# One core, attention and two feed-forward stages: the attention loop's scans, gate logits, row scatters and last two tiles put in another order and on other engines

## The chip, the cores and the metric

The kernel runs on one core of a Trainium2 chip. The metric is the device time of one execution in microseconds (us): 826.85 us before the change, median of 3 runs (826.71 to 828.07). The engines are TensorE (PE, with PEld for its weight loads), VectorE (DVE), ScalarE (ACT), GpSimd (POOL) and SyncE (SP, which only issues transfers here). Each runs its own instructions in order and waits on semaphores.

## The reference

A recurrent attention with per-channel decay is followed by a mixture of experts with one expert for each token, and that by a dense feed-forward layer. Cut to what matters:

```python
batch, n_heads, seq, head_dim = (4, 8, 768, 48)
for t in range(S):                       # w is drawn from 0.8 to 0.95
    cur = np.einsum('bhd,bhe->bhde', u[None] * kt, vt)
    y[:, :, t] = np.einsum('bhd,bhde->bhe', rt, state + cur)
    state = wt[:, :, :, None] * state + np.einsum('bhd,bhe->bhde', kt, vt)
x = y as (3072 tokens, 384)
logits = x @ w_gate;  e_idx = argmax(logits);  gate_w = softmax(logits)[e_idx]
eom = sigmoid(x @ w_output_gate)
out[token] = gate_w * eom[e_idx] * (relu(x @ w1[e_idx]) @ w2[e_idx])
h = out @ w_in;  result = (h * clip(h + 3, 0, 6) / 6) @ w_out
```

## The kernel before

**Stage one, attention.** The sequence is cut into chunks of 128 steps, and each chunk of one batch entry is a *tile*: 24 tiles (NT), numbered so that tile i continues tile i-4 (B = 4). In a tile the 8 heads lie in 4 pairs (PR = 4), a pair on 112 partitions. One load brings `a` (w with a zero column ahead of each pair's 128, then r, then k) and one brings `v`.

The recurrence of a chunk becomes matrix products. DVE scans w backward to R (`prep_a`: the product of all decays behind a step; its column 0 is the decay of the whole chunk) and forward to Fx. Before the forward scan the reciprocals of column 0 of R are put into the marks `mk_f`, so that Fx carries 1/(whole decay). GpSimd forms kh = k times R (`prep_k`), m = r times k (`prep_m`), sb = the carried state T times the decay; DVE forms rh = r times Fx (`prep_b`). Then PE makes scores `sc` from kh and rh (`scores`), DVE copies the causal part of them over the diagonal matrix A (two masked copies, L456), PE multiplies A by v and adds rh times sb (`ymm`, tile `yp`), ACT copies that out as `ys`. The state update goes over `kt` (a transpose, tile `kp`, copied to `ks` by ACT) and `upd` (tile `up`, then T on DVE).

**Gate and scatter.** `small_a` multiplies ys and m by the gate weights for all four pairs (`lt`, copied to `lts`), `small_b` transposes that (`lp`); DVE takes the diagonal terms `av` from it (L534), from which GpSimd makes the A of the next tile (affine select, L536), and sums the 16 logits over the pairs into `L` (L543). When a group of 4 (later 2) tiles is complete, some 16 small DVE instructions (`gate_steps`, `gate_pb`, `gate_b`) find each token's expert, its row there (`pi`) and its factor (`sg`). Then for each tile of the group PE transposes ys (`rows_pe`), GpSimd writes a token number (`rows_id`), ACT scales by sg into `xs` (`rows_act`, L640), and GpSimd issues an indirect transfer of the 128 rows to `x_w` in memory (`scatter`, L647). `clear` zeroes a window of `x_w` for each expert beforehand.

**The loop.** Step i prepares tile i+2, makes scores of tile i, `ymm` of tile i-1, logits of tile i-2. The order is written by hand (a manual schedule). Small gate instructions are woven into the next step by `tick`. PSUM tags are single buffers: `k` serves kp, up and lp; `x` serves the busy matmuls, lt and row transposes; `y` serves yp; `s0` and `s1` serve the scores. A matmul into a tag waits until the earlier tenant has been read. A *step* below runs from one backward scan (L392) to the next; step i scans tile i+2, so the scan of tile 23 begins step 21. After the loop the last tiles, two gates and eight scatters are written out by hand. In between, the weights of the first expert are split (`piece_hi` on ACT, `piece_lo` on DVE, 16 of each).

**Stages two and three** (experts, dense layer) start when all scatters have landed and the first window of `x_w` is loaded: the transposes at L872. From there PE is busy to the end. No instruction of these stages is changed.

Of the kernel before, what the change touches and what calls it, by code (L numbers as in the profile page):

```python
# [7 lines left out]
F32 = mybir.dt.float32  # L8
# [12 lines left out]
C = 128  # L21
# [191 lines left out]
def kernel(  # L213
# [33 lines left out]
    wg_sb = ca.tile([PP, 2, PR, 32], F32, name="wg_sb")  # L247
    rev8_s = ca.tile([128, E], F32, name="rev8_s")
# [114 lines left out]
    nc.gpsimd.memset(b_lo, W_LO)  # L363
# [21 lines left out]
    def prep_a(i):  # L385


        d = tl[i]
        tick()
        a = d["a"]  # L390
        R = wk.tile([PP, PR * SEG], F32, tag="R", name="R", bufs=3)
        nc.vector.tensor_tensor_scan(out=R[:, ::-1], data0=a[:, 1:1 + PR * SEG][:, ::-1], data1=mk_r[:, ::-1],  # L392
                                     initial=0.0, op0=ALU.mult, op1=ALU.max)
        tick()
        nc.vector.reciprocal(out=mk_f[:, 0:PR * SEG:SEG], in_=R[:, 0:PR * SEG:SEG])
        tick()
        Fx = wk.tile([PP, PR * SEG], F32, tag="F", name="Fx", bufs=3)
        nc.vector.tensor_tensor_scan(out=Fx, data0=a[:, 0:PR * SEG], data1=mk_f,
                                     initial=0.0, op0=ALU.mult, op1=ALU.add)
        tick()  # L400
        d["R"], d["F"] = (x.rearrange("p (a b) -> p a b", b=SEG) for x in (R, Fx))
# [126 lines left out]
    def small_b(i, j, lts):  # L528
        lp = ps_o.tile([128, 128], F32, tag="k", name="lp")
        nc.tensor.transpose(out=lp, in_=lts, identity=ident)  # L530
        lq = lp.rearrange("t (p q) -> t q p", p=PR)
        if j < NT:
            av = wk.tile([128, 2, PR], F32, tag="av", name="av")
            nc.vector.tensor_copy(av, lq[:, 16:18, :])  # L534
            A = wk.tile([128, 2, PR, C], F32, tag="A", name="A", bufs=4)
            nc.gpsimd.affine_select(out=A, in_=av.unsqueeze(3).to_broadcast([128, 2, PR, C]), pattern=[[0, 2], [0, PR], [1, C]],  # L536
                                    compare_op=ALU.is_equal, fill=0.0, base=0, channel_multiplier=-1)
            tl[j]["A"] = A
        if 0 <= i < NT:
# [690 lines left out]
```

## Time and profile before

| | |
|---|---|
| median of 3 runs | 826.85 us (826.71 to 828.07) |
| the profiled execution | 828.91 us |
| its span, first to last instruction | 827.1 us (1.8 us lie around it) |
| busy: PE, DVE, ACT, POOL | 781.5, 489.8, 351.0, 167.5 us |
| first transposes of stage two | 194.12 us after the span's start |

The profile is one execution. A row of its timeline gives start and duration of instructions of one line, the number of them merged, and in brackets the idle time of the engine before, with what ended it. Busy times of PE are modelled and overlap; durations of steps are therefore read from starts.

### The profile page before, as it was taken

Reading aid. Unit: us, or ns where it says so; the run is one execution under the profiler, and the core shown is the slowest. Engines: PE = TensorE matmul, PEld = TensorE weight load, DVE = VectorE, ACT = ScalarE, POOL = GpSimd, SP = SyncE. Lnnn points to the kernel's source line nnn. Section 1 sums busy time; section 2 is a strip of 40 time slices with the busy share of each in tenths; the row PEclk is TensorE's granted clock in tenths of the full one; section 3 lists DMA queues with packets and bytes.
Section 4 is the critical chain, followed back from the end, with each engine's and each line's share of the span. In section 5 each row is a group of like instructions: output and inputs, shape, how many; then the busy total and the mean of one; then the engine's idle time right before and its main releaser. Section 6 shows DMA issues by size and latency. Waiting matters only on the chain.

```text
span 827.1 us, 13670 instructions
## 1 busy us (share of the span) xinstructions
PE 781.5 (94%) x5349; PEld 694.3 (84%) x5359; DVE 489.8 (59%) x993; ACT 351.0 (42%) x671; POOL 167.5 (20%) x240
## 2 busy tenths in 40 slices
PE   6789989888999999999899999999999999999996
PEld 3567767667999999989889899999999999999995
DVE  7989999843776877787777633433343343343332
ACT  3445555532545555464554533333333333333332
POOL 5657888745000000000000020001002002002002
PEclk9999999989999999999999999999999999999998
DMA  9996675114568777575522010000001001001001
GB/s 248 295 284 193 187 205 163 41 68 158 190 184 214 179 261 208 169 155 195 148 84 59 1 38 2 1 4 35 0 1 39 1 2 38 1 1 39 1 1 42
DMA packets 31867, 85.47 MB, mean 103 GB/s; under 512 B 6521, under 2 KB 17985, under 8 KB 31793
## 3 DMA queue, kind: packets, MB, share of 16 engines
q1 hardware_dynamic: 28721, 75.05, 31.5%
q0 software_dynamic: 3072, 9.45, 3.1%
q8 instruction: 44, 0.72, 0.4%
q14 instruction: 30, 0.25, 0.1%
HBM read 67.11 MB, written 17.39 MB: 102 GB/s over the span
## 4 chain that ended last, share of the span: by engine, by line
PE 48%; issue 32%; DVE 10%; DMA 3%; POOL 3%; ACT 2%; SPq 0%; POOLq 0%; ACTq 0%; DVEq 0%
PE hp L879 6%; PE hp L880 6%; PE hp L881 6%; PE yp L880 3%; PE yp L879 3%; PE yp L881 3%; PE op L881 3%; PE op L880 3%; PE op L879 3%; PE yp L492 2%; POOL out_dram L1116 2%; PE sc L445 2%; DVE A L456 2%; PE yp L497 2%; DVE wlo L345 2%
## 5 line engine op out<-in xcount | busy, mean ns | idle before, releaser
L1030 DVE SCALAR_TENSOR_TENSOR t<-t,hp 128x512 f32<-128x512 f32 x96 | 66.0, 687 | 161.0 <-ACT t L1029 161.0
L1116 POOL DMA_INDIRECT out_dram<-ob,ids_sb x24 | 24.7, 1030 | 595.6 <-ACT ob L1114 590.5
L1029 ACT ACTIVATE t<-hp,b 128x512 f32<-128x512 f32 x96 | 65.9, 686 | 160.4 <-PE hp L881 153.9
L879 PE MATMUL op<-whi,hhi 128*128 128x384 f32 x380 | 128.4, 338 | 0.0
L880 PE MATMUL op<-wlo,hhi 128*128 128x384 f32 x380 | 128.3, 338 | 0.0
L881 PE MATMUL op<-whi,hlo 128*128 128x384 f32 x380 | 128.1, 337 | 0.0
L879 PE MATMUL hp<-xhi,win_hi 128*128 128x512 f32 x288 | 112.7, 391 | 1.9 <-ACT xhi L1017 1.9
L880 PE MATMUL hp<-xlo,win_hi 128*128 128x512 f32 x288 | 113.8, 395 | 0.4 <-DVE xlo L1018 0.4
L881 PE MATMUL hp<-xhi,win_lo 128*128 128x512 f32 x288 | 112.8, 392 | 0.0
L1036 DVE TENSOR_TENSOR hlo<-t,hhi 128x512 fp32r<-128x512 f32 x95 | 65.8, 693 | 66.3 <-ACT hhi L1035 66.3
L1035 ACT ACTIVATE hhi<-t 128x512 fp32r<-128x512 f32 x95 | 60.0, 632 | 72.2 <-DVE t L1030 72.2
L879 PEld LDWEIGHTS op<-whi,hhi 128*128 128x128 f32 x380 | 71.3, 188 | 4.1
L880 PEld LDWEIGHTS op<-wlo,hhi 128*128 128x128 f32 x380 | 71.2, 187 | 3.7
L345 DVE TENSOR_TENSOR wlo<-raw,whi 128x384 fp32r<-128x384 f32 x144 | 74.1, 551 | 0.0
L321 ACT ACTIVATE whi<-raw 128x768 fp32r<-128x768 f32 x64 | 53.9, 843 | 42.6 <-DMA raw<-in_w_dram 30.3
L881 PEld LDWEIGHTS op<-whi,hlo 128*128 128x128 f32 x380 | 71.2, 187 | 0.2 <-DVE hlo L1036 0.2
L879 PE MATMUL yp<-hhi,whi 128*128 128x360 f32 (+6 forms) x192 | 65.0, 339 | 3.1 <-ACT yst L1065 3.1
L879 PE MATMUL hp<-xhi,whi 128*128 128x360 f32 (+6 forms) x186 | 64.9, 349 | 0.5 <-ACT xhi L858 0.5
L880 PE MATMUL yp<-hlo,whi 128*128 128x360 f32 (+6 forms) x192 | 65.0, 339 | 0.1
L881 PE MATMUL yp<-hhi,wlo 128*128 128x360 f32 (+6 forms) x192 | 65.0, 339 | 0.0
L881 PEld LDWEIGHTS hp<-xhi,win_lo 128*128 128x128 f32 x288 | 54.1, 188 | 11.8
L880 PE MATMUL hp<-xlo,whi 128*128 128x360 f32 (+6 forms) x186 | 63.1, 339 | 0.8 <-DVE xlo L859 0.8
(169 smaller groups left out, 1405.2 us busy)
## 6 DMA issues: line engine op xcount, KB each, us to landing
raw<-in_w_dram SPq DMA_DIRECT2D x32, 768.0 KB, 5.3
a<-in_att_dram SPq DMA_DIRECT2D x23, 675.5 KB, 5.8
raw<-in_wout_dram SPq DMA_DIRECT2D x16, 384.0 KB, 6.8
raw<-in_win_dram SPq DMA_DIRECT2D x16, 384.0 KB, 4.5
v<-in_tok_dram SPq DMA_DIRECT2D x24, 192.0 KB, 9.6
wo_d<-v SPq DMA_DIRECT2D x16, 192.0 KB
raw<-wo_d SPq DMA_DIRECT2D x4, 768.0 KB, 4.1
xw<-x_w SPq DMA_DIRECT2D x4, 576.0 KB, 5.6
```

The costliest lines, as they stand in the source:

```text
L321: nc.scalar.activation(out=chunks[key][0][:, sl], in_=raws[key][:, sl], func=AF.Copy)
L345: nc.vector.tensor_tensor(out=lo[:, sl], in0=raws[key][:, sl], in1=hi[:, sl].bitcast(F32), op=ALU.subtract)
L445: nc.tensor.matmul(out=scs[hf][:, p, :], lhsT=kh[r0:r0 + D, p, :], rhs=rh[r0:r0 + D, p, :], start=True, stop=True)
L456: nc.vector.copy_predicated(out=d["A"][:, hf], mask=mask.unsqueeze(1).to_broadcast([128, PR, C]), data=scs[hf])
L879: nc.tensor.matmul(out=out_ap, lhsT=lh, rhs=rh, start=first, stop=False)
L880: nc.tensor.matmul(out=out_ap, lhsT=lh, rhs=rl, start=False, stop=False)
L881: nc.tensor.matmul(out=out_ap, lhsT=ll, rhs=rh, start=False, stop=last)
L1029: nc.scalar.activation(out=t, in_=hp, func=AF.Relu, bias=b_3)
L1030: nc.vector.scalar_tensor_tensor(out=t, in0=t, scalar=6.0, in1=hp, op0=ALU.min, op1=ALU.mult)
L1035: nc.scalar.activation(out=hi, in_=t, func=AF.Copy)
L1036: nc.vector.tensor_tensor(out=lo, in0=t, in1=hi.bitcast(F32), op=ALU.subtract)
L1116: ins = nc.gpsimd.indirect_dma_start(out=out, out_offset=bass.IndirectOffsetOnAxis(ap=ids_sb[:, i:i + 1], axis=0), in_=ob, in_offset=None)
```

## The change

The change touches stage one only.

- One tile of marks serves both scans: 1e-25, and 1.0 at the segment borders, shifted by a column for the forward scan, which now takes the maximum where it added. It no longer carries 1/(whole decay); its result `Fp` lies in PSUM. The reciprocals go to a small tile `rt`, and ACT multiplies r by them (`prep_s`, four activations of 128 columns, one for each pair). `rh` is the product of that (`rs`) and `Fp`.
- The logits and diagonal terms come from one matmul of lts with a constant `sel` (24 columns) in place of the transpose; it goes to tag `y`, and ACT copies it out. The DVE copy and reduction of `small_b` are gone.
- The lower check of w reads column 0 of R (4 columns) where it read 512 columns of w.
- `kt` is issued ahead of `prep_b`; scatters of a tile are issued right behind its rows, ahead of the affine select (`diag`); 3 busy matmuls stand in a gate step.
- The clears stand in steps 1 to 6 (two in each of steps 4 and 5) where they stood in 0 to 7; the raw weight loads and the splits by piece stand in other steps.
- The loop ends one step earlier, and the rest has a new order.

```diff
-    mk_r, mk_f = (vtile(PR * SEG)[0:PP] for _ in range(2))
+    marks = vtile(PR * SEG + C)[0:PP]
+    mk_r, mk_f = marks[:, 0:PR * SEG], marks[:, C:C + PR * SEG]
+    Fp = vtile(PR * SEG)[0:PP]
...
-        nc.vector.reciprocal(out=mk_f[:, 0:PR * SEG:SEG], in_=R[:, 0:PR * SEG:SEG])
+        nc.vector.reciprocal(out=rt, in_=d["R"][:, :, 0])
...
-        nc.vector.tensor_tensor_scan(out=Fx, data0=a[:, 0:PR * SEG], data1=mk_f,
-                                     initial=0.0, op0=ALU.mult, op1=ALU.add)
+        nc.vector.tensor_tensor_scan(out=Fp, data0=d["a"][:, 0:PR * SEG], data1=mk_f,
+                                     initial=0.0, op0=ALU.mult, op1=ALU.max)
...
+        for p in range(PR):
+            nc.scalar.activation(out=rs[:, p, :], in_=d["a"][:, WM + p * C:WM + (p + 1) * C], func=AF.Copy, scale=d["rt"][:, p:p + 1])
...
-        nc.vector.tensor_tensor(out=rh, in0=a[:, WM:WM + PR * C].rearrange("p (a b) -> p a b", b=C),
-                                in1=Fx[:, :, 0:C], op=ALU.mult)
+        nc.vector.tensor_tensor(out=rh, in0=d["rs"], in1=Fp.rearrange("p (a b) -> p a b", b=SEG)[:, :, 0:C], op=ALU.mult)
...
-        nc.tensor.transpose(out=lp, in_=lts, identity=ident)
...
-            nc.vector.tensor_copy(av, lq[:, 16:18, :])
...
-            nc.vector.tensor_reduce(out=gd[g]["L"][:, z, :], in_=lq[:, 0:2 * E, :], axis=AX.X, op=ALU.add)
+        lp = ps_o.tile([128, 24], F32, tag="y", name="lp")
+        nc.tensor.matmul(out=lp, lhsT=lts, rhs=sel, start=True, stop=True)
...
+        nc.scalar.activation(out=lq, in_=lp, func=AF.Copy)
...
-        if 0 <= i < E:
-            clear(i)
+        for e in CLEARS.get(i, ()):
+            clear(e)
...
-        keep_busy(NWARM[i + 3] if i < 2 else 1, ps_o, "x")
+        keep_busy(NWARM[i + 3] if i < 2 else 3 if gb is not None else 1, ps_o, "x")
...
+        av = small_v(i - 2, i + 1, small_p(lts)) if lts is not None else None
+        for z in range(0 if i < E else 1 if i < 20 else 2):
             if todo:
                 j = todo.pop(0)
-                rows_pe(j, ("x", "s1")[z])
+                rows_pe(j, ("x", "k")[z])
                 rows_id(j)
                 rows_act(j)
-                sq.append(j)
+                scatter(j)
...
+        if av:
+            diag(*av)
```

Where the instructions stand, on DVE, in step 12 of the loop, before (the row names a line, an operation, output and inputs; `vps` is the PSUM tile of the marks):

```order
L392 SCALAR_TENSOR_TENSOR R<-a,vps 112x516
L395 RECIPROCAL vps<-R 112x4
L398 SCALAR_TENSOR_TENSOR Fx<-a,vps 112x516
L456 COPY_PREDICATED A<-mask,sc_1392 128x512
L456 COPY_PREDICATED A<-mask,sc_1393 128x512
L422 TENSOR_TENSOR rh<-a,Fx 112x512
L480 TENSOR_TENSOR T<-up,sb 112x192
L345 TENSOR_TENSOR wlo<-raw,whi 128x384
L534 COPY av<-lp 128x8
L543 TENSOR_REDUCE vps<-lp 128x16
```

The same step on DVE with the change (`vps` now also holds Fp):

```order
L399 SCALAR_TENSOR_TENSOR R<-a,vps 112x516
L407 RECIPROCAL rt<-R 112x4
L409 SCALAR_TENSOR_TENSOR vps<-a,vps 112x516
L475 COPY_PREDICATED A<-mask,sc_1437 128x512
L475 COPY_PREDICATED A<-mask,sc_1438 128x512
L441 TENSOR_TENSOR rh<-rs,vps 112x512
L499 TENSOR_TENSOR T<-up,sb 112x192
L352 TENSOR_TENSOR wlo<-raw,whi 128x384
```

The last two rows are gone, and rh reads one operand from PSUM and one that ACT wrote.

On ACT, a step before, from the copy of kp on:

```order
L464 ACTIVATE ks<-kp 128x448
L500 ACTIVATE ys<-yp 112x512
L525 ACTIVATE lts<-lt 128x128
L640 ACTIVATE xs<-xp,sg 128x384
L435 ACTIVATE junk,wchk<-a,b_lo 112x512
L435 ACTIVATE junk,wchk<-a,b_hi 112x512
L340 ACTIVATE whi<-raw 128x384
```

And with the change:

```order
L483 ACTIVATE ks<-kp 128x448
L434 ACTIVATE rs<-a,rt 112x128 x4
L519 ACTIVATE ys<-yp 112x512
L544 ACTIVATE lts<-lt 128x128
L561 ACTIVATE L<-lp 128x24
L672 ACTIVATE xs<-xp,sg 128x384
L454 ACTIVATE junk,wchk<-R,b_lo 112x4
L454 ACTIVATE junk,wchk<-a,b_hi 112x512
L347 ACTIVATE whi<-raw 128x384
```

Five activations more stand in the step, four of them between ks and ys, and the first check is 4 columns wide.

On POOL, a step before (`gap` is a small write behind each scatter):

```order
L414 TENSOR_TENSOR kh<-a,R 112x512
L407 TENSOR_TENSOR m<-a 112x512
L427 TENSOR_TENSOR sb<-T,R 112x192
L633 COPY xs<-tokid 128x1
L536 AFFINE_SELECT A<-av 128x1024
L647 DMA x_w<-xs,pi 24576x385
L285 MEMSET gap 1x1
```

And with the change:

```order
L425 TENSOR_TENSOR kh<-a,R 112x512
L418 TENSOR_TENSOR m<-a 112x512
L445 TENSOR_TENSOR sb<-T,R 112x192
L665 COPY xs<-tokid 128x1
L679 DMA x_w<-xs,pi 24576x385
L292 MEMSET gap 1x1
L567 AFFINE_SELECT A<-L 128x1024
```

The affine select that makes the next tile's A now stands behind the scatter; in steps 20 and 21 it stands behind two of them.

## Rows read from the trace of the kernel before

**Rows 1.** Busy time by stretch: us, PE, PEld, DVE, ACT, POOL, PEclk, DMA share, GB/s.
```profile
13.66:64.52 50.86, 40.29 (x571) 30.71 (x578) 45.01 (x91) 22.69 (x59) 30.77 (x31) 0.90 0.97 285
64.52:132.00 67.48, 62.41 (x921) 47.79 (x920) 64.70 (x134) 36.95 (x92) 56.99 (x69) 0.97 0.68 189
132.00:154.87 22.87, 20.04 (x270) 15.30 (x268) 21.05 (x60) 12.48 (x35) 16.93 (x23) 0.90 0.32 103
154.87:194.12 39.25, 32.53 (x316) 22.48 (x315) 18.88 (x81) 12.02 (x31) 23.98 (x42) 0.89 0.22 77
```

**Rows 2.** Timeline of DVE: a gate step begins at 77.35, step 12 at 92.01.
```profile
77.35 1.22 DVE L392 TENSOR_TENSOR_SCAN R<-a,vps 112x516 f32<-112x516 f32 x1
...
85.72 1.20 DVE L392 TENSOR_TENSOR_SCAN R<-a,vps 112x516 f32<-112x516 f32 x1
...
92.01 1.23 DVE L392 TENSOR_TENSOR_SCAN R<-a,vps 112x516 f32<-112x516 f32 x1
...
97.97 0.15 DVE L534 COPY av<-lp 128x8 f32<-128x8 f32 x1
...
98.30 1.23 DVE L392 TENSOR_TENSOR_SCAN R<-a,vps 112x516 f32<-112x516 f32 x1
```

**Rows 3.** Timeline of PE, from logits transpose to logits transpose, one step.
```profile
97.59 0.33 PE L530 MATMUL lp<-ident,lts 128*128 128x128 f32 x1 [0.15 <-DVE T L480]
97.85 1.16 PE L445 MATMUL sc<-rh,kh 48*128 48x128 f32 x16
...
103.88 0.33 PE L530 MATMUL lp<-ident,lts 128*128 128x128 f32 x1 [0.16 <-DVE T L480]
```

**Rows 4.** The line of rh: duration ns min/median/max, first and last start.
```profile
L422 DVE TENSOR_TENSOR rh<-a,Fx x24: 661/921/1545, 7.1 to 158.7; 112x512 f32<-112x512 f32 x24
```

**Rows 5.** The same for the state update, one of whose inputs lies in PSUM.
```profile
L480 DVE TENSOR_TENSOR T<-up,sb x16: 340/349/358, 42.1 to 145.5; 112x192 f32<-112x192 f32 x16
```

**Rows 6.** Groups by line on DVE: rh in 13.66 to 64.52, then in 64.52 to 132.00.
```profile
L422 DVE TENSOR_TENSOR rh<-a,Fx 112x512 f32<-112x512 f32 x8 | 7.0, 870 | 0.0
...
L422 DVE TENSOR_TENSOR rh<-a,Fx 112x512 f32<-112x512 f32 x10 | 11.3, 1126 | 0.0
```

**Rows 7.** Waits of DVE, 13.66 to 64.52: us in total, times, longest.
```profile
DVE av L534 <- PE lp L530: 3.3, 7, 0.5
...
DVE R L392 <- DMA a<-in_att_dram: 0.4, 1, 0.4
```

**Rows 8.** Timeline of ACT: copies of 512 and 128 columns, scalings of 384.
```profile
95.33 0.60 ACT L500 ACTIVATE ys<-yp 112x512 f32<-112x512 f32 x1 [1.09 <-PE yp L497]
96.38 0.28 ACT L525 ACTIVATE lts<-lt 128x128 f32<-128x128 f32 x1 [0.45 <-PE lt L522]
97.48 0.58 ACT L640 ACTIVATE xs<-xp,sg 128x384 f32<-128x384 f32 x1 [0.82 <-PE xp L628]
...
159.81 1.05 ACT L640 ACTIVATE xs<-xp,sg 128x384 f32<-128x384 f32 x2 [0.74 <-PE xp L628]
```

**Rows 9.** Timeline of POOL: the issue of one scatter in step 12.
```profile
93.18 1.05 POOL L647 DMA_INDIRECT x_w<-xs,pi  x1 [0.17 <-POOL A L536]
```

**Rows 10.** Timeline of PE: twelve busy matmuls at the end of stage one.
```profile
183.72 2.99 PE L374 MATMUL wp<-busy,ones_b 128*128 128x512 bf16 x12 [0.27 <-DVE pb L607]
```

**Rows 11.** Timeline of the end of stage one: PE, POOL.
```profile
173.33 1.09 PE L492 MATMUL yp<-A,v 128*64 128x128 f32 x16
...
187.34 0.96 POOL L647 DMA_INDIRECT x_w<-xs,pi  x1 [0.22 <-issue]
...
194.12 0.83 PE L872 MATMUL xp<-ident,xw 128*128 128x128 f32 x6 [0.23 <-DMA xw<-x_w]
```

**Rows 12.** Timeline of DVE and ACT there: the last tile's A, its ys.
```profile
169.11 1.34 DVE L456 COPY_PREDICATED A<-mask,sc 128x512 f32<-128x512 int32 x2
...
176.80 0.60 ACT L500 ACTIVATE ys<-yp 112x512 f32<-112x512 f32 x1 [1.56 <-PE lp L530]
```

**Rows 13.** Timeline of PE in step 11, after a gate step: the same products at another clock.
```profile
85.78 1.97 PE L492 MATMUL yp<-A,v 128*64 128x128 f32 x16
```

More of the change, by code (lines that the diff above doesn't have):

```diff
@@ L247 @@
     wg_sb = ca.tile([PP, 2, PR, 32], F32, name="wg_sb")
+    sel = ca.tile([128, 24], F32, name="sel")
     rev8_s = ca.tile([128, E], F32, name="rev8_s")
@@ L680 @@
             small_b(-1, 0, lts0)
-        for j in [i + 2] if i + 2 < NT else []:
-            prep_a(j)
+        if i + 2 < NT:
+            j = i + 2
+            prep_r(j)
+            prep_f(j)
             if i == -1:
@@ L690 @@
             scores(i)
-        for j in [i + 2] if i + 2 < NT else []:
+        if 0 <= i < NT - B:
+            kt(i)
+        if i + 2 < NT:
+            prep_s(j)
             prep_b(j)
@@ L716 @@
             gate_pb(gb)
-        if 7 <= i < 23:
-            piece_lo((0, (i - 7) // 4), (i - 7) % 4)
-        if lts is not None:
-            small_b(i - 2, i + 1, lts)
+        if av:
+            diag(*av)
+        for _ in range(PIECES.count(i - 1)):
+            q, r = next(los)
+            piece_lo((0, q), r)
         if i >= 2:
@@ L728 @@
             gb = None
-        while sq:
-            scatter(sq.pop(0))
         if 0 <= i + 2 < NT:
             wcheck(i + 2)
-        if 6 <= i < 22:
-            piece_hi((0, (i - 6) // 4), (i - 6) % 4)
+        for _ in range(PIECES.count(i)):
+            q, r = next(his)
+            piece_hi((0, q), r)
     G = len(grp) - 1
-    assert ga is None and gb is None and GROUPS[-2:] == [2, 2]
-    tags = ["s0", "s1"] * 4
-    def scat_rows(j):
-        rows_act(j)
-        scatter(j)
-    assert len(todo) == 3
@@ new lines, in gate_2 @@
+    def gate_2(g, tag):
+        gate_exp(g)
+        gate_pe(g, tag)
+        gate_pb(g)
+        gate_b(g)
+    scores(a)
+    for _ in gate_steps(G - 2):
+        pass
+    ymm(a - 1)
+    lts = small_a(a - 2, b)
+    rows_to(todo[0], "k")
+    diag(*small_v(a - 2, b, small_p(lts)))
+    scatter(todo[0])
+    lts = small_a(a - 1, NT)
+    gate_2(G - 2, "k")
+    scores(b)
+    small_v(a - 1, NT, small_p(lts))
+    rows_to(todo[1], "k")
+    scatter(todo[1])
+    for _ in gate_steps(G - 1):
+        pass
@@ L780 @@
+    ymm(a)
+    ymm(b, "s0")
+    lts = small_a(a, NT)
+    gate_2(G - 1, "k")
+    rows_to(a - 4, "s1")
+    scatter(a - 4)
+    small_v(a, NT, small_p(lts))
+    rows_to(a - 3, "k")
+    scatter(a - 3)
+    lts = small_a(b, NT)
+    small_v(b, NT, small_p(lts))
+    for _ in gate_steps(G):
+        pass
+    rows_to(a - 2, "s1")
+    scatter(a - 2)
+    rows_to(a - 1, "k")
+    scatter(a - 1)
+    gate_exp(G)
+    rows_pe(a, "s0")
+    rows_pe(b, "s1")
     gate_pe(G, "y")
@@ L782 @@
     gate_b(G)
-    scat_rows(NT - 2)
-    scat_rows(NT - 1)
-    keep_busy(TAILB[1], ps_o, "y")
+    for j in (a, b):
+        rows_id(j)
+        rows_act(j)
+        scatter(j)
+    for q, r in los:
+        piece_lo((0, q), r)
+    keep_busy(TAILB, ps_o, "k")
     assert len(scat) == NT
```

125 lines of the change are left out of this document (57 added, 68 removed).

## Prediction

> **What bounds the kernel now.** I read the busy times of the stretches first, because the change sits in stage one only. [Rows 1] cut that stage at the backward scans of tiles 2, 10, 20 and 23 and at stage two's first transposes: steps 0 to 7 (50.86 us), 8 to 17 (67.48 us), 18 to 20 (22.87 us) and the last tiles (39.25 us), 180.46 us in all. The reader is to see that DVE is busy 64.70 of 67.48 us in the second stretch, PE 62.41 and POOL 56.99: DVE paces, with two engines close behind it. In the first stretch DVE is busy 45.01 of 50.86 us and the DMA share is 0.97. In the last nothing is full; there a chain of waits decides.
>
> The timeline of DVE shows what a step consists of. Step 12 takes 98.30 - 92.01 = 6.29 us and a gate step 85.72 - 77.35 = 8.37 us [rows 2]. The reader is to see that the copy of av begins at 97.97 and the next scan at 98.30: 0.33 us of each step belong to the logits.
>
> The line of rh has 24 instances of one shape between 661 and 1545 ns [rows 4]: something holds it up. T, which also multiplies or adds two tensors but has one of them in PSUM, stays within 340 to 358 ns over 16 instances, amid the same GpSimd work [rows 5].
>
> Then PE, the next limit: from one logits transpose to the next 103.88 - 97.59 = 6.29 us, of which it waited 0.16 for T; its own work is 6.13 us, of which the transpose's slot is 97.85 - 97.59 = 0.26 us [rows 3].
>
> **The change part by part.**
>
> *Logits off DVE.* Copy and reduction go: 0.33 us a step [rows 2]; in steps 0 and 1 only the copy exists, which I count at 0.1. In steps 0 to 7 DVE also stood idle 3.3 us in 7 waits for the transpose [rows 7]; with nothing behind lp on DVE these waits go. On PE the transpose of 128 columns becomes a product with 24: between 0.26 x 24/128 = 0.05 us and the old 0.26. I take 0.13, nearer the lower end, because a weight load stays. On ACT one copy of 24 columns comes: below the 0.28 us of 128 columns [rows 8].
>
> *rh with one input in PSUM.* I take 0.67 us, the undisturbed instance of the same shape. In steps 0 to 7 the 8 instances took 7.0 us, in 8 to 17 the 10 took 11.3 [rows 6]: 7.0 - 5.4 = 1.6 and 11.3 - 6.7 = 4.6 us. The other bound is that nothing is saved, if a PSUM input were no shelter; the T of [rows 5] is why I take the first. The Trainium skill (SBUF — State Buffer, Who interferes with whom) says that a DVE instruction with two SBUF inputs contends with a GpSimd instruction that reads SBUF, since its second input comes over an interface the two share; by it rh leaves the contention, as the rows suggest, and without it both savings would be nil.
>
> *Scans, reciprocals, marks.* As many, of the same sizes. That the forward scan writes PSUM has no row; it could cost or save a little, I take nothing.
>
> *r scaled by ACT.* Four activations of 128 columns with a scale for each partition. The nearest row has 384 columns and takes 0.58 us alone, 1.05 for two, so 0.47 for a following one; a column costs (0.60 - 0.28)/384 = 0.83 ns by the copies of 512 and 128 [rows 8]. So 256 columns less: 0.37 us for the first, 0.26 for the others, 1.15 us in all (between 4 x 0.11 for columns alone and 4 x 0.37). The cover is the forward scan and two masked copies, some 2.5 us between the reciprocal and rh on DVE. If ACT came late, DVE would wait at rh, and T, the pieces and the next scan with it. The narrower check gives back some 0.43 us of ACT. Its busy time was 36.95 of 67.48 us [rows 1], 3.7 us a step; it becomes about 4.7, below PE's 6.0.
>
> *Scatter ahead of the affine select.* A(i+1) now waits for xs(i), an issue of 1.05 us and a gap [rows 9]. PE ends the rows about when the next step's scores begin; 0.65 us later xs is there, 1.2 later the affine select starts, and 1.1 later A is ready: 3 us into the step, while DVE reaches A's masked copy 2.7 us into its own. So it costs nothing while PE paces; POOL's work for a step is unchanged.
>
> *Busy matmuls.* Twelve took 2.99 us [rows 10]: 0.25 each, 0.5 more in a gate step.
>
> *Clears and raw loads later.* In all the bytes are the same. Up to the scan of tile 10 there must land 11 loads of a (0.69 MB) and v (0.20) and 7 clears (0.60 on average), 14.0 MB; some 3 were there by 13.66. The other 11 MB at 285 GB/s [rows 1] need 39 us.
>
> *sel at the start.* A reduction waits on DVE ahead of the first scan for the identity. Its cover is the load of tile 2, which that tile's scan awaits anyway [rows 7].
>
> Now by stretch. **Steps 0 to 7:** logits 6 x 0.33 + 0.2 = 2.2, waits 3.3, rh 1.6: 7.1 us less, 43.8 left, above the 39 us of the transfers.
>
> **Steps 8 to 17:** DVE would fall by 4.6 + 3.3, and by 1.0 since 8 pieces lie there for 10: to 58.6 us. But then PE paces: 6.13 - 0.13 = 6.0 a step, and in the two gate steps 0.5 of busy matmuls and some 0.15 of rank products, which PE already had: 60.0 + 1.3 = 61.3 us. I take PE's figure: 6.2 us less. A gate step is longer than 6.0 on DVE, but its surplus is worked off in the next steps, because PE reaches the next scores only when it has done its own step.
>
> **Steps 18 to 20:** two gates in three steps, DVE paces; logits 1.0, rh 0.3, against a piece more (0.5) and two gate instructions (0.4) that before lay ahead of step 18: 0.4 us less.
>
> **Hand-overs:** with PE, DVE and POOL all near full, I add 0.05 us to each of 21 steps: 1.05 us.
>
> **The last tiles:** A(22) comes later (its affine select stands behind two scatters in step 21, 2 x 1.2 us), but before it waited for scores, and A(23) stays within a microsecond of its old distance. Behind A(23), which began at 169.11 and took 1.34 us [rows 12], the products of tile 23 began only at 173.33 [rows 11]: 2.9 us behind it, after another tile's logits and two row transposes. Now they follow the products of tile 22 directly, about 0.6 us behind A(23): 2.3 less. ys then started at 176.80 [rows 12], 1.4 us after the products' end; now nothing stands ahead of it: 1 less. Together with A(23)'s 0.6, some 3.9 less. Against that, PE waits around there: after such a pause 16 products took 1.97 us [rows 13] for 1.09 [rows 11], nearly twice as long, as at the lower of the two clock levels, and the products of two tiles would then cost up to 3.7 more. I take 2.2 less, between 0 and 4.
>
> The sum: 7.1 + 6.2 + 0.4 - 1.05 + 2.2 = 14.85 us. The profiled execution took 828.91 us, which is 2.06 above the median: 828.91 - 14.85 - 2.06 = **812.0 us**.
>
> **The rivals.**
>
> *A fuller gain* (15%): no loss at hand-overs (1.05), the last tiles at the higher clock (1.7 more), and more of the idle time of the first stretch gone (5.85 us idle, of which I counted 3.3): 2 more. 812.0 - 4.7 = 807 us.
>
> *Transfers pace the first steps* (9%). For: a share of 0.97 over the whole first stretch [rows 1], and two clears in each of steps 4 and 5. Against: 39 us needed, 43.8 there. If other queues' packets slow it by a sixth, 3 us are lost: 815 us.
>
> *GpSimd paces* (10%): the scatter waits for xs with kh, m and the affine select queued behind it. For: 56.99 of 67.48 us busy [rows 1]; if a step stays at 6.29 on POOL, the middle saves some 3 us where I count 6.2, and the next stretch nothing: 816 us.
>
> *Slower: rs comes late on every step* (6%). The place is DVE's rh, behind the fourth activation, which stands behind ks, which waits for kt. The loop T, kt (0.6), ks (0.55), rs (1.15), rh (0.67), T (0.35) is 3.3 us and has room in 6. It decides once rs ends 0.7 us after the masked copies in 22 steps (15 us); at 1.2 us the time is 812 + 26 = 838 us. The Trainium skill's advice speaks for this rival (ScalarE: Activation LUTs, Rules for kernel authors: multiplications belong on VectorE). ACT's rows, 36.95 of 67.48 us [rows 1], speak against it.
>
> *The change does little* (6%): PE, now the pace, drops to its lower clock after gate steps as in [rows 13], where 16 products lost 0.9 us; a whole step would lose some 4, and three such stretches would take 12 us back: 824 us.
>
> **How the numbers follow.** The forecast has 54%, with a range of its own from 808 to 817. For 8 in 10 I reach to 803 (the fuller gain with rounding) and 821 (GpSimd's case with the last tiles giving nothing, 818, and a part of the clock's). A difference of 0.2%, 1.7 us, is about what a measurement of this kernel tells from no change. Faster by more: the forecast, the fuller gain, transfers, GpSimd and nearly all of the clock's case, less mishaps that I can't name: 0.88. Same 0.05, slower 0.07.
>
> **What would show it.** In the changed profile the scan of tile 10 should begin near 58 us and that of tile 23 near 142; rh should stay near 0.67 us; DVE should show idle time in steps 8 to 17, ended by PE (scores or up), and PE's step should be about 6.0 us; stage two's first transposes should begin near 179.3. Four activations of rs should take 1.1 to 1.2 us and DVE should not wait for them. I am wrong if rh varies as before, if DVE's idle time is ended by rs, if POOL is busy throughout, or if PE's granted clock stands well below 0.97 in the middle.

## The result: 1.1% slower, and where the time went

The changed kernel takes 834.01 us (median of 8 runs) beside 825.77 us for the kernel before (8 runs): ratio 1.0108, 95% interval 1.0078 to 1.0137. The prediction said 812.0. In a second comparison (after_again, below) the ratio was 1.0071 (1.0043 to 1.0098). The profiled execution took 834.41 us with a span of 832.7, so it stands 5.5 us above the profiled execution of before.

The busy times of the changed kernel in the stretches of [rows 1], cut at the same scans and at the second group of stage two's transposes (the row at 194.12 in [rows 11], which the prediction called the first, is the second group as well):

```profile
13.36:58.95 45.59, 41.98 (x595) 32.31 (x597) 40.28 (x75) 28.96 (x97) 31.64 (x31) 0.93 1.00 288
58.95:130.82 71.87, 65.36 (x904) 50.71 (x900) 58.93 (x110) 44.62 (x138) 50.71 (x66) 0.91 0.69 188
130.82:157.22 26.40, 21.91 (x297) 16.89 (x296) 25.18 (x57) 17.01 (x54) 19.12 (x27) 0.93 0.30 99
157.22:195.79 38.57, 31.69 (x306) 21.93 (x304) 18.01 (x76) 13.66 (x40) 23.89 (x40) 0.87 0.27 93
```

The first number behind a stretch is its length. Against [rows 1], in us:

| stretch | before | after | measured | predicted |
|---|---|---|---|---|
| steps 0 to 7 | 50.86 | 45.59 | -5.27 | -7.1 |
| steps 8 to 17 | 67.48 | 71.87 | +4.39 | -6.2 |
| steps 18 to 20 | 22.87 | 26.40 | +3.53 | -0.4 |
| last tiles | 39.25 | 38.57 | -0.68 | -2.2 |
| hand-overs | | | | +1.05 |
| stage two to the end | 632.98 | 636.91 | +3.93 | 0 |
| start to the scan of tile 2 | 13.66 | 13.36 | -0.30 | 0 |

The gain of the first stretch is there, and the two in the middle lose it again. DVE's timeline shows the first cause: the scans of tiles 10, 11 and 12 wait 9.46 us for `a`. In the kernel before none of these three waited, and DVE waited for a load once in the whole first stretch, 0.4 us [rows 7].

```profile
58.95 1.23 DVE L399 TENSOR_TENSOR_SCAN R<-a,vps 112x516 f32<-112x516 f32 x1 [1.95 <-DMA a<-in_att_dram]
...
67.80 1.23 DVE L399 TENSOR_TENSOR_SCAN R<-a,vps 112x516 f32<-112x516 f32 x1 [4.20 <-DMA a<-in_att_dram]
...
75.75 1.23 DVE L399 TENSOR_TENSOR_SCAN R<-a,vps 112x516 f32<-112x516 f32 x1 [3.31 <-DMA a<-in_att_dram]
```

SyncE's queue shows why. Its rows are issues, with the time that each took:

```profile
36.05 6.18 SPq L686 DMA_DIRECT2D x_w<-zero  x2
...
42.39 3.19 SPq L304 DMA_DIRECT2D a<-in_att_dram  x1
...
48.84 0.46 SPq L320 DMA_DIRECT2D raw<-in_w_dram  x1
...
55.08 0.33 SPq L320 DMA_DIRECT2D raw<-in_w_dram  x1
...
56.22 0.33 SPq L304 DMA_DIRECT2D a<-in_att_dram  x1
```

Two clears of one step took 6.18 us to issue. The load of tile 10 stood behind them: it was issued at 42.39 and landed at 58.93. The loads of tiles 11 and 12 were issued at 50.28 and 56.22, each behind a load of raw weights of 0.79 MB.

The second cause stands in gate step 14, here on DVE:

```profile
104.80 2.00 DVE L603 TENSOR_TENSOR vps<-L,O 128x32 f32<-128x32 f32 x1
...
106.72 0.72 DVE L475 COPY_PREDICATED A<-mask,sc 128x512 f32<-128x512 int32 x1
...
109.31 2.42 DVE L352 TENSOR_TENSOR wlo<-raw,whi 128x384 fp32r<-128x384 f32 x2
```

and on GpSimd at the same time:

```profile
104.34 1.18 POOL L425 TENSOR_TENSOR kh<-a,R 112x512 f32<-112x512 f32 x1
...
105.48 1.26 POOL L418 TENSOR_TENSOR m<-a 112x512 f32<-112x512 f32 x1
...
109.72 1.12 POOL L567 TENSOR_SCALAR_AFFINE_SELECT A<-L 128x1024 f32<-128x1024 f32 x1
```

The product of logits and marks (L603), 128 x 32 elements, lasts 2.00 us and ends with GpSimd's m, at 106.7 to 106.8. Further down two weight pieces take 2.42 us where a single one took 0.54 to 0.60 before; GpSimd's affine select begins 0.41 us behind the first of them. By line, over the whole kernel (min/median/max in ns), first the product in the kernel before, then the product and rh in the changed one; rh was to be cured, and is [rows 4]:

```profile
L571 DVE TENSOR_TENSOR vps<-vps,O x8: 182/191/200, 51.9 to 181.6; 128x32 f32<-128x32 f32 x4, 128x16 f32<-128x16 f32 x4
...
L603 DVE TENSOR_TENSOR vps<-L,O x8: 182/556/2035, 47.8 to 183.0; 128x32 f32<-128x32 f32 x4, 128x16 f32<-128x16 f32 x4
...
L441 DVE TENSOR_TENSOR rh<-rs,vps x24: 662/670/687, 7.9 to 160.9; 112x512 f32<-112x512 f32 x24
```

The change had moved the logits `L` from PSUM to SBUF, since ACT writes them there for the affine select to read. So the product, like rh before, had two inputs in SBUF while GpSimd ran, and lo_psum below shows that this is what held it: with one of them in PSUM it takes 180 to 197 ns. That is the rule of the Trainium skill (SBUF — State Buffer, Who interferes with whom) that the prediction had cited for rh: a DVE instruction with two SBUF inputs contends with a GpSimd instruction that reads SBUF. The prediction had not asked which other instruction the change puts in that position.

In the last tiles a masked copy waits 4.76 us for an affine select that stands behind two scatters on GpSimd:

```profile
163.56 1.05 POOL L679 DMA_INDIRECT x_w<-xs,pi  x1 [0.98 <-ACT xs L672]
...
165.11 0.98 POOL L679 DMA_INDIRECT x_w<-xs,pi  x1 [0.28 <-POOL xs L665]
...
166.14 1.11 POOL L567 TENSOR_SCALAR_AFFINE_SELECT A<-L 128x1024 f32<-128x1024 f32 x1
```

```profile
167.28 1.33 DVE L475 COPY_PREDICATED A<-mask,sc 128x512 f32<-128x512 int32 x2 [4.76 <-POOL A L567]
```

And PE is at the lower of its two levels (1.2 of 2.4 GHz; the granted clock is 0.50) in two places around the end of stage one: from 170.4 to 177.1, with the products of tile 22 (16 in 1.97 us; those of tile 23 took 1.09 before [rows 11]), and from 197.7 to 201.0, with the first products of stage two, 0.33 us apart:

```profile
172.48 1.97 PE L511 MATMUL yp<-A,v 128*64 128x128 f32 x16
...
176.26 1.52 PE L511 MATMUL yp<-A,v 128*64 128x128 f32 x16
...
195.79 0.83 PE L922 MATMUL xp<-ident,xw 128*128 128x128 f32 x6 [0.53 <-DMA xw<-x_w]
...
198.36 0.54 PE L964 MATMUL hp<-xhi,whi 128*128 128x400 f32 x1
198.70 0.54 PE L965 MATMUL hp<-xhi,wlo 128*128 128x400 f32 x1
```

In the middle it was at 0.50 from 71.4 to 78.1, where DVE waited for the load of tile 12, and from 109.0 to 115.7, in gate step 14; so the mean of steps 8 to 17 is 0.91, where it was 0.97.

### The profile page after: what moved, and what is told of

It reads as the page before. It is cut to its first block, busy times and chain, and to the rows that moved or that the text cites. A ratio compares the mean times of both kernels' runs of the same rounds, so it can differ in the third digit from the quotient of the medians.

```text
span 832.7 us, 13826 instructions
## 1 busy us (share of the span) xinstructions
PE 792.0 (95%) x5393; PEld 702.2 (84%) x5393; DVE 482.2 (58%) x946; ACT 373.2 (45%) x794; POOL 164.0 (20%) x240
## 4 chain that ended last, share of the span: by engine, by line
PE 36%; issue 33%; DVE 12%; DMA 10%; POOL 5%; ACT 3%; SPq 0%; POOLq 0%; ACTq 0%; DVEq 0%
PE hp L929 5%; PE hp L930 4%; PE hp L931 4%; DMA raw<-in_w_dram 4%; DMA a<-in_att_dram 4%; DVE wlo L352 3%; POOL out_dram L1166 2%; PE op L931 2%; PE op L930 2%; PE op L929 2%; PE yp L929 2%; PE yp L930 2%; PE yp L931 2%; PE yp L511 2%; PE sc L464 2%
## 5 line engine op out<-in xcount | busy, mean ns | idle before, releaser
L352 DVE TENSOR_TENSOR wlo<-raw,whi 128x384 fp32r<-128x384 f32 x144 | 76.7, 571 | 0.0
```

The source lines that it names most:

```text
L352: nc.vector.tensor_tensor(out=lo[:, sl], in0=raws[key][:, sl], in1=hi[:, sl].bitcast(F32), op=ALU.subtract)
```

## The experiments

Each ratio is to the kernel before on the same chip; on the four chips used it took 831.3, 835.3, 833.7 and 827.0 us. A profile is one execution, and stage two, whose instructions no edit touches, differs by up to 10 us between profiles. So the edits are compared by their ratios, and, inside stage one, by the start of the scan of tile 23. That start is no exact measure either: it was 157.22 and 160.57 in two profiles of the changed kernel.

### One edit at a time

**raws_later.** The raw weights come later.

```diff
-RAWS = [6, 7, 15, 18]
+RAWS = [8, 11, 15, 18]
```

> The changed kernel, with the first two weight loads (raw, 0.79 MB each) issued in steps 8 and 11 instead of 6 and 7, so behind the loads of tiles 12 and 15; nothing else. Theory (transfers pace steps 6 to 10): DVE's waits for a at the scans of tiles 10, 11 and 12, 9.5 us in the changed kernel, fall by 1.57 MB at some 270 GB/s, 5.8 us, and the time by about 5, to 829. Rival one (the two clears a step fill the queue, not the weights): the waits stay above 7 us, time within 2 of 834. Rival two (the waits are slack of a step that another engine paces): the waits go and the time stays.

**clears_only.** The clears as before, the weights left where the change put them.

```diff
-CLEARS = {1: (0,), 2: (1,), 3: (2,), 4: (3, 4), 5: (5, 6), 6: (7,)}
+CLEARS = {e: (e,) for e in range(8)}
```

> The changed kernel with one clear in each of steps 0 to 7, as in the kernel before; the weights stay in steps 6 and 7. Theory (bytes ahead of the loads of tiles 10 to 12 count, whichever they are): a clear more lands in the free first steps, the two-clear issues of 5.7 to 6.2 us go, DVE's waits for a at tiles 10 to 12 fall from 9.5 by some 2 to 3 us; ratio 1.005. Rival one (only the weights matter): waits within 1 us of 9.5. Rival two (the doubled clears are the whole cause): waits under 2 us.

Measured: ratios 1.0103 (1.0063 to 1.0143) and 1.0070 (1.0042 to 1.0098). Neither can be told from the changed kernel's own 1.0108 and 1.0071. The waits went all the same. DVE's timeline with the weights later (the scan of tile 12 has no wait any more):

```profile
60.10 1.23 DVE L399 TENSOR_TENSOR_SCAN R<-a,vps 112x516 f32<-112x516 f32 x1 [1.74 <-DMA a<-in_att_dram]
...
65.53 1.23 DVE L399 TENSOR_TENSOR_SCAN R<-a,vps 112x516 f32<-112x516 f32 x1 [0.78 <-DMA a<-in_att_dram]
...
74.07 2.36 DVE L603 TENSOR_TENSOR vps<-L,O 128x32 f32<-128x32 f32 x1
```

and with the clears as before (all the waits of these tiles; the copy at 71.33 belongs to tile 9):

```profile
65.67 1.23 DVE L399 TENSOR_TENSOR_SCAN R<-a,vps 112x516 f32<-112x516 f32 x1 [0.66 <-DMA a<-in_att_dram]
...
71.33 1.34 DVE L475 COPY_PREDICATED A<-mask,sc 128x512 f32<-128x512 int32 x2 [3.09 <-POOL A L567]
...
74.18 1.23 DVE L399 TENSOR_TENSOR_SCAN R<-a,vps 112x516 f32<-112x516 f32 x1 [0.67 <-DMA a<-in_att_dram]
...
77.91 1.28 DVE L603 TENSOR_TENSOR vps<-L,O 128x32 f32<-128x32 f32 x1
```

Either edit takes the waits at tiles 10 to 12 from 9.46 us to 2.5 and 1.3, so it was neither the clears nor the weights alone. Tiles 11 and 12 gain by either edit; the wait at tile 10 hardly changes when the weights come later (1.74 us after 1.95) and goes with single clears.

Of the 6.9 and 8.1 us of waits that went, 1.9 and 1.1 us are left as gain at the scan of tile 20 (it begins at 128.97 and 129.71, 130.82 in the changed kernel). A part of the rest went to the product in gate step 10 (74.07 and 77.91), which grew from 0.51 us to 2.36 and 1.28. In the changed kernel GpSimd had been idle while DVE waited for its load, began kh as soon as R was there and had done m at 79.46, when the product began at 79.48. With the load in time, GpSimd's scatter and affine select came first, and kh or m ran beside the product. In raws_later T then waited 1.28 us for PE in step 11. In clears_only a scatter, with the affine select for the copy at 71.33 behind it, began 3 us behind the end of its xs. The semaphores in the trace show what held it: GpSimd waited until 67.85 for the last clear, issued at 52.20, whose last part landed at 67.83. A scatter writes the memory that the clears zero, and with one clear a step the last clear is issued later (47.52 in the changed kernel).

These two ratios do not measure stage one alone: in the profile of raws_later stage two's second transposes begin 4 us sooner than in the changed kernel's (191.84 for 195.79), and from the first copy hhi to the first store it is 3.2 us longer.

**lo_psum.** A second copy of the marks goes to PSUM, and the product reads that one.

```diff
+        o2 = q["o2"].rearrange("t (j e) -> t j e", e=E)[:, 0:n]
+        V.tensor_tensor(out=o2, in0=i8, in1=m8.unsqueeze(2).to_broadcast([128, n, E]), op=ALU.is_equal)
-        V.tensor_tensor(out=lo, in0=d["L"][:, 0:n, E:2 * E], in1=O, op=ALU.mult)
+        V.tensor_tensor(out=lo, in0=d["L"][:, 0:n, E:2 * E], in1=o2, op=ALU.mult)
```

> The changed kernel, with a second copy of the marks O of each gate written to PSUM (one more DVE instruction of about 0.19 us in a gate), so that the product of logits and marks reads one input from SBUF and one from PSUM; nothing else. Theory (two inputs in SBUF hold it while GpSimd's kh and m run): it falls from 2.0 us to about 0.19 in the gate steps 14, 18 and 20, each of these steps gets some 1.7 us shorter, 5 in all: 829. Rival (DVE only waits elsewhere, PE or GpSimd pace the gate steps): the product is short, but the steps lose under 0.5 us each and the time stays within 1.5 of 834.

Ratio 1.0029 (1.0001 to 1.0058). The product's line is now

```profile
L605 DVE TENSOR_TENSOR vps<-L,vps x8: 180/188/197, 48.1 to 173.1; 128x32 f32<-128x32 f32 x4, 128x16 f32<-128x16 f32 x4
```

and gate steps 14, 18 and 20 last 8.78, 8.31 and 8.30 us after 11.84, 11.34 and 10.04; the scan of tile 23 begins at 150.33 instead of 157.22. In steps 14 and 18 that is more than the products' own 1.8 us: with DVE ahead, the pieces there no longer ran beside the affine select and took 0.55 us each.

**before_L_sbuf.** The reverse, in the kernel before.

```diff
-                gd[g]["L"] = gps[g % 2]["L"].rearrange("t (j e) -> t j e", e=2 * E)
+                gd[g]["L"] = sm.tile([128, 4, 2 * E], F32, tag="L", name="L")
```

> The kernel before, with the sums of the logits written to an SBUF tile instead of PSUM; nothing else. Theory: the product of logits and marks, 0.18 to 0.20 us in all 8 gates before, now lasts until GpSimd's kh and m end, up to 2 us in the gates of the scan steps, and as DVE paces there the time rises by 1.5 us for each of 3 to 5 gates, 4 to 8 us: 830 to 834. Rival (the place of L has nothing to do with it): 0.2 us as before, time 826.

Ratio 1.0120 (1.0085 to 1.0155). The mechanism is there, the size is not. In gate step 18

```profile
136.42 0.84 DVE L564 TENSOR_TENSOR df<-L,mx 128x32 f32<-128x32 f32 x1
...
139.32 0.41 DVE L571 TENSOR_TENSOR vps<-L,O 128x32 f32<-128x32 f32 x1
```

the product takes 0.41 us, not 2 (before: 0.20), and df, which also had both inputs in SBUF here, 0.84 (before 0.17 to 0.19). df ended with GpSimd's affine select (136.10 to 137.20), the product with kh (138.48 to 139.67), and was let in ahead of m. Why the changed kernel's product was not, I can't say. The scan of tile 23 was 7.7 us later than in the first profile of before, more than these rows account for (0.9 us for each of 5 gates). Most of the rest stands in steps 11 and 19, each behind a gate step, where T waited 2.09 and 1.92 us for PE and the granted clock was 0.68 and 0.73 (0.77 and 0.78 before). Whether that follows from the longer gate steps no run shows.

**scatter_behind.** The scatters behind the affine select again.

```diff
                 rows_act(j)
-                scatter(j)
+                sq.append(j)
...
+        while sq:
+            scatter(sq.pop(0))
         if 0 <= i + 2 < NT:
             wcheck(i + 2)
```

> The changed kernel with the scatters of a step issued behind the affine select again, as in the kernel before; nothing else. Theory (the scatter's wait for xs holds the affine select, which then runs beside the weight pieces of a gate step and holds them): the pieces in gate steps 14 and 18 fall from 1.95 and 1.90 us to 0.55, DVE's waits for A (0.8 to 1.0 us in steps 13, 14, 16 and 17 or so) go, the scan of tile 23 comes 4 to 6 us sooner, ratio 1.005. Rival (only the order of two instructions with one total): waits for A stay, the scan of tile 23 within 1 us of 157.

Beside it the changed kernel ran once more on the same chip:

> The changed kernel as it is, beside the others on one chip, since stage two's first experts differed by several us between profiles of kernels that share its code. Theory: ratio to before 1.011 as at first. Rival (part of the first ratio was such a difference): nearer to 1.005.

Ratios 1.0002 (0.9972 to 1.0032) and, for the changed kernel, 1.0071 (1.0043 to 1.0098), between its two expectations; the scan of tile 23 at 155.52 and 160.57. In gate step 14

```profile
109.77 1.22 DVE L603 TENSOR_TENSOR vps<-L,O 128x32 f32<-128x32 f32 x1
...
113.50 1.01 DVE L352 TENSOR_TENSOR wlo<-raw,whi 128x384 fp32r<-128x384 f32 x2
```

the two pieces take 1.01 us, and the product 1.22: it was held by m alone, which began 0.13 us ahead of it. DVE's waits for A in steps 8 to 17, 3.5 us in 4 waits in the changed kernel, are gone, and that in the last tiles falls from 4.76 to 1.26 us. Steps 13 to 20, which take 62.2 and 62.1 us in the two profiles of the changed kernel, take 55.5.

### Edits together

**raw_lo** is raws_later with lo_psum; **raw_lo_scatter** has scatter_behind as well; **raw_lo_clears** is raw_lo with the clears of clears_only; **raw_lo_pct** has, beyond that, the weight pieces outside of the three gate steps and the order of tail_rank (below).

> Both edits of raws_later and lo_psum. Theory (late loads and held products are two separate losses, and the second hit gate step 10 as soon as the loads no longer delayed it): DVE's waits for a at tiles 10 to 12 under 3 us as in raws_later, gate step 10 near 8.0 us instead of 10.0, the scan of tile 23 near 144 (157.2 in the changed kernel, 150.3 and 155.4 with one edit), ratio 0.995. Rival (stage two waits for its weights and takes the gain back): the scan of tile 23 near 144 too, but ratio 1.00 or above, with the first experts longer by what stage one saved.

> All three edits (weights in steps 8 and 11, the product from PSUM, scatters behind the affine select). Theory: with the loads in time, the product short and the affine select early, DVE's full steps are paced by PE near 6.0 us or by DVE near 5.4; the scan of tile 23 at 140 to 142, which is where the prediction had it, ratio 0.99. Rival (stage two takes it back): the same scan, ratio 1.00.

> Weights in steps 8 and 11, the product from PSUM, and one clear a step from step 0. Theory: what is left of DVE's waits for a (3.9 us at tile 10 and 0.9 at tile 11 with the first two edits) falls under 2 us, the scan of tile 23 at 144 to 145 after 147.5. Rival (the transfers as a whole are late, in whichever order): waits near 4 us, the scan at 147.

> As raw_lo_clears, with the weight pieces kept out of gate steps 14, 18 and 20 (PIECES 10, 11, 11, 12, 14, 14, 15, 15, 16, 16, 18, 18, 20, 20, 21, 21) and the rank products of tail_rank. Theory: the gate steps lose their pieces, 0.55 us each (5 of them), and full steps take them while PE or GpSimd pace, so the scan of tile 23 is 2 us sooner than in raw_lo_clears, and the end 1.5 us more: ratio 0.985. Rival (full steps have no room, two pieces in one step run beside GpSimd's work and are held): the scan no sooner.

| kernel | ratio | 95% interval | scan of tile 23 |
|---|---|---|---|
| raw_lo | 0.9901 | 0.9867 to 0.9934 | 147.47 |
| raw_lo_scatter | 0.9886 | 0.9846 to 0.9925 | 146.89 |
| raw_lo_clears | 0.9871 | 0.9837 to 0.9904 | 141.58 |
| raw_lo_pct | 0.9911 | 0.9878 to 0.9943 | 141.13 |

Two edits, of which one alone gave nothing that can be measured and the other less than 1%, together take 1% off the kernel before and nearly 2% off the changed one. raw_lo's scan came at 147.5, not at the expected 144, with 4.8 us of waits for loads left; with the clears back these went too, and the scan came at 141.6, sooner than the expected 144 to 145. raw_lo_scatter missed its expectation of 140 to 142: beside raw_lo it gains 0.6 us at the scan, and its ratio can't be told from raw_lo's. In steps 13 to 20 it is even 2.0 us longer (55.1 for 53.1): with the product short, the scatters behind the affine select bring nothing. The pieces outside of gate steps gained nothing: the gate steps got 0.3 to 0.8 us shorter, and the full steps, where the second of two pieces was held (0.86 us), took that back.

The best of them ran again, beside the kernel before with a profile on that chip:

> The kernel of the three edits (weights in steps 8 and 11, the product from PSUM, one clear a step), once more. Theory: ratio 0.987 again; the scan of tile 23 at 142; hhi to the first store within 2 us of the kernel before on this chip. Rival: hhi to the first store 5 us or more above the kernel before on this chip, which would put stage two's share of the lost gain on the change.

> The kernel before as it is, profiled on the chip of the next two. Theory (stage two's first experts take longer on these chips for every kernel): from the first copy hhi to the first store of the output 296 to 299 us as in the edited kernels, where the first profile had 291.1. Rival (the changed order of stage one makes stage two wait for weights): 291 to 293.

816.39 us against 826.98, ratio 0.9875 (0.9836 to 0.9915). Its stretches, cut as above:

```profile
14.43:57.88 43.45, 39.47 (x552) 30.21 (x553) 40.40 (x77) 27.39 (x93) 30.41 (x30) 0.88 1.00 293
57.88:120.47 62.59, 61.16 (x930) 47.47 (x930) 55.63 (x113) 45.98 (x143) 52.14 (x67) 1.00 0.78 219
120.47:142.09 21.62, 20.05 (x299) 15.46 (x295) 20.39 (x60) 16.87 (x54) 17.84 (x26) 1.00 0.36 112
142.09:180.87 38.78, 30.14 (x305) 20.93 (x301) 18.95 (x79) 13.60 (x41) 24.42 (x40) 0.91 0.28 97
```

Steps 0 to 7 take 43.45 us (predicted 43.8), steps 8 to 17 62.59 (61.3), steps 18 to 20 21.62 (22.5). In steps 8 to 17 PE's clock is 1.00, and PE is busy for 61.16 of 62.59 us. Stage two's length is read from the first copy hhi

```profile
186.78 1.05 ACT L952 ACTIVATE hhi<-hp 128x400 fp32r<-128x400 f32 x2 [3.74 <-PE hp L971]
```

to the first store of the output

```profile
477.44 0.97 POOL L1168 DMA_INDIRECT out_dram<-ob,ids_sb  x1 [291.62 <-ACT ob L1166]
```

That is 290.66 us, and 290.77 in the kernel before on this chip (196.63 to 487.40). The other profiles, with the same instructions there, have 291 to 300.5 us. So the expectation of 296 to 299 for the kernel before failed, and no part of this length is shown to come from the change.

### Terms and misses

**fp_sbuf.** raw_lo_clears with the forward scan's result in SBUF, so rh has two inputs there.

```diff
-        nc.vector.tensor_tensor_scan(out=Fp, data0=d["a"][:, 0:PR * SEG], data1=mk_f,
+        Fx = wk.tile([PP, PR * SEG], F32, tag="F", name="Fx", bufs=1)
+        d["F"] = Fx
+        nc.vector.tensor_tensor_scan(out=Fx, data0=d["a"][:, 0:PR * SEG], data1=mk_f,
```

> The kernel of the three edits with the forward scan written to an SBUF tile, so that rh reads both inputs from SBUF; nothing else. Theory (an input in PSUM is what shelters rh): rh goes from 0.67 us in all 24 instances to a mean of 0.9 to 1.1, and as DVE, PE and GpSimd are near one another in steps 8 to 17, the scan of tile 23 comes 3 to 6 us later; ratio 0.992. Rival one (the shorter rh came from r being scaled by ACT or from a different order): rh stays near 0.67. Rival two (rh is held, but PE paces): the scan within 1 us of 142.

Ratio 0.9941 (0.9906 to 0.9976), the scan of tile 23 at 148.87. The group of rh in steps 8 to 17, and that of raw_lo_clears_2 under it:

```profile
L443 DVE TENSOR_TENSOR rh<-rs,Fx 112x512 f32<-112x512 f32 x10 | 12.1, 1212 | 0.0
```

```profile
L441 DVE TENSOR_TENSOR rh<-rs,vps 112x512 f32<-112x512 f32 x10 | 6.7, 668 | 0.0
```

So the input in PSUM is what shelters rh, and here that is worth 6.8 us at the scan of tile 23.

**tail_rank.** The changed kernel, with the rank products of the last but one gate between the products of the last two tiles.

```diff
     ymm(a)
-    ymm(b, "s0")
-    lts = small_a(a, NT)
     gate_2(G - 1, "k")
     rows_to(a - 4, "s1")
     scatter(a - 4)
+    ymm(b, "s0")
+    lts = small_a(a, NT)
```

> The changed kernel with the rank products of the last but one gate, and what follows from them up to tile 18's scatter, put between the products of tiles 22 and 23 instead of behind both; nothing else. Theory (GpSimd's last six scatters, 1.48 us apart, pace the end, and the first of them waited 6.03 us for xs behind those products): the row of scatters starts 2.5 us sooner, stage two's first transposes 1.5 to 2 us sooner behind the scan of tile 23 (37.1 us in the changed kernel). Rival (the last gate sets the end): within 0.5 us of 37.1.

Ratio 1.0155 (1.0121 to 1.0189): the theory fell. Tile 18's scatter came sooner (3.63 us of wait instead of 6.03), but the next one waited again and the last began 34.1 us behind the scan of tile 23 (157.93), 2.4 later than in the changed kernel:

```profile
179.51 0.98 POOL L679 DMA_INDIRECT x_w<-xs,pi  x1 [3.63 <-issue]
...
184.71 0.98 POOL L679 DMA_INDIRECT x_w<-xs,pi  x1 [4.00 <-ACT lts L544]
...
192.06 0.98 POOL L679 DMA_INDIRECT x_w<-xs,pi  x1 [0.28 <-POOL xs L665]
```

PE did the products of tile 23 at the lower clock as well,

```profile
178.02 1.97 PE L511 MATMUL yp<-A,v 128*64 128x128 f32 x16
...
179.92 1.72 PE L516 MATMUL yp<-rh,sb 48*48 48x128 f32 x16
```

1.97 and 1.72 us where the changed kernel had 1.52 and 1.08.

**busy28.** 28 busy matmuls ahead of stage two instead of 20 (`NBUSY`).

> The changed kernel, with 28 busy matmuls instead of 20 ahead of stage two, 8 x 0.22 = 1.8 us more of PE work in the pause before the first window. Theory (the pause of 1.82 us put PE to its lower clock, at which stage two's first products came 0.33 us apart instead of 0.18): the first hhi copy, 7.5 us behind the first transposes' start in the changed kernel, comes 1.5 us sooner after it, time about 832.5. Rival (transfers of the window set it, the clock would have fallen anyway): no change, 834; if the busy matmuls run over the window's arrival, up to 0.5 more.

Ratio 1.0166 (1.0119 to 1.0213): this theory fell too. PE had no pause between the busy matmuls and the first transposes, and the products were 0.33 us apart nevertheless. Behind the transposes PE still waited 0.63 and 0.59 us; in the kernel before, whose products were 0.18 us apart, it waited 0.23 and 0.60 there.

```profile
193.21 6.20 PE L383 MATMUL wp<-busy,ones_b 128*128 128x512 bf16 x28 [0.25 <-DVE flag_f L861]
...
203.26 0.54 PE L964 MATMUL hp<-xhi,whi 128*128 128x400 f32 x1
...
203.59 0.54 PE L965 MATMUL hp<-xhi,wlo 128*128 128x400 f32 x1
```

What sets the clock there is left open.

## Why the prediction was wrong

The measured change of the span is +5.6 us, the predicted one -14.85: 20.45 us to account for. Two steps of the prediction failed and carry most of it: the count of what must land ahead of tile 10's scan, and the product of logits and marks, for which the prediction had no term.

*The logits, the waits for lp, rh* (steps 0 to 7, predicted -7.1): right. The stretch lost 5.27 us in spite of a wait of 1.95 us for tile 10's load; without that, 7.2. rh is 662 to 687 ns in all 24 instances, four rs take 1.28 us, and DVE waited for them 1.0 us in all, in tiles 0 and 1. fp_sbuf shows that the PSUM input is the reason for rh.

*"The other 11 MB at 285 GB/s [rows 1] need 39 us"*: this step failed, and with it 9.46 us. It counted what must land ahead of tile 10's scan, 14.0 MB in all, as if the queue served that first. By the packets in the trace 16.1 MB had moved when the load landed at 58.93, 0.77 MB of them weights that were issued behind it; and it was issued late, behind two clears. And the step stopped at tile 10, where the weights of steps 6 and 7 stand ahead of the loads of tiles 11 and 12. The rival that transfers pace the first steps had the mechanism, with a third of the price and the wrong place.

*Steps 8 to 17* (predicted -6.2, measured +4.39): 7.51 us are the waits at tiles 11 and 12; 3.2 us are the product (2.00 for 0.20) and the held piece (1.95 for 0.55) in gate step 14. Without these 10.7 us the stretch would by this sum have been 6.3 us shorter. PE as the next pace, at 61.3 us, fits raw_lo_clears_2, where the stretch takes 62.59 and PE is busy for 61.16. But DVE's waits there were ended by GpSimd's affine select in the main (4.6 us from step 8 on, for PE 0.8), and not by PE as the prediction said.

*Steps 18 to 20* (-0.4, +3.53): two products held (1.82 and 1.85 us) and a piece (1.35), 5.0 us. The prediction put this at nothing: it moved L to SBUF without asking who reads it. lo_psum shows the share of the products.

*"So it costs nothing while PE paces"* (the scatter ahead of the affine select): the condition failed. PE did not pace in the changed kernel (busy for 65.36 of 71.87 us in steps 8 to 17); there A came 0.8 to 1.0 us late in 4 full steps, the affine select ran beside the pieces of steps 14 and 18, and scatter_behind makes steps 13 to 20 6.6 us shorter. With the weights later and the product mended the sentence fits: raw_lo and raw_lo_scatter differ by 0.6 us at the scan of tile 23.

*PE's clock.* The prediction named a clock well below 0.97 in the middle as a sign of being wrong, and it was 0.91. In raw_lo_clears_2, without the waits and the held product, it is 1.00; so here the low clock came with them.

*The last tiles* (-2.2, -0.68): A(22) waited 4.76 us for its affine select, but A(23) began 14.39 us behind the scan of tile 23, 14.24 before, as the prediction had it. What failed is "about 0.6 us behind A(23)": the products of tile 23 began 3.33 us behind its end, since those of tile 22 had only just begun, at the lower clock. The prediction had named this clock as up to 3.7 us against its gain of 3.9, and put 1.7 of them into the sum. Two profiles of one kernel, raw_lo_clears and raw_lo_clears_2, show both cases:

| profile | 16 products of tile 22 | tile 23's products behind A(23) | last tiles |
|---|---|---|---|
| before_again | 1.09 | 2.81 | 36.29 |
| changed kernel | 1.97 | 3.33 | 38.57 |
| lo_psum | 1.09 | 0.52 | 35.27 |
| raw_lo_clears | 1.09 | 0.53 | 35.75 |
| raw_lo_clears_2 | 1.97 | 3.61 | 38.78 |

So the shorter way is there when the clock holds, and which case comes no run explains. The base is soft as well: the last tiles of the kernel before took 39.25 us in the profile of [rows 1], with PE at the lower level from 177.4 to 184.2, and 36.29 in before_again, without that.

*Stage two* (0, +3.93): 1.6 us are its first products at the lower clock (the first hhi copy begins 6.01 us behind the second transposes, 4.44 before). The rest lies within what the same instructions differ by between profiles.

With the loads and the product mended, the prediction's markers are met up to the last tiles: the scan of tile 10 at 57.88 (near 58), that of tile 23 at 142.09 (near 142). The second transposes come at 180.87 (179.3). The last tiles are 2.5 us longer than in the kernel before on that chip, where 2.2 less were forecast; these 4.7 us are about what lies between the 10.6 us gained there and the 14.85 forecast.

## What to carry to other kernels

When a change moves a tile from PSUM to SBUF, look up every instruction that reads it, and count how many of its inputs then lie in SBUF, with what GpSimd runs beside it. When loads are moved, follow the queue up to the last tile that could be late, and see how long SyncE takes to issue: in the changed kernel the late loads went on for two tiles past the one that the prediction had counted. One mended cause may show nothing, since the next takes its place: here raws_later and clears_only took away about 7 and 8 us of waits and no time that their ratios can tell, and raws_later together with lo_psum took 1% off the kernel before.

## What the hardware showed unexpectedly

- A small DVE instruction with two inputs in SBUF was held through two GpSimd instructions in a row, kh and m, to the end of the second (2.00 us for 0.20 of work, 2.36 in raws_later), and in before_L_sbuf only through kh.
- One clear mostly took 0.8 to 1.0 us to issue. Two in a row took 1.6 us the first time and 6.18 the second, in a stretch with a DMA share of 1.00, and the load behind them another 3.19.
- 28 busy matmuls with no pause between them and the transposes did not keep PE at its higher clock for the products that followed (busy28).
- One and the same kernel had its last tiles at the higher clock in one profile and at the lower in another, 35.75 and 38.78 us.
